# Keys on GpSimd's queue, SyncE in text order from the last q, k, v chunk on, and two low parts on GpSimd, in a gated mix of attention and MLP

## The chip, the cores and the metric

The kernel runs on one core of one Trainium2 chip. The metric is the device time of one execution in microseconds (us), smaller is better. TensorE is called PE below, VectorE DVE, ScalarE ACT, GpSimd POOL and SyncE SP. SP computes nothing here: it issues DMAs, one after the other, and where one of them has to wait, all behind it wait too. POOL both computes and issues DMAs.

## The reference

One layer norm and MLP and one attention block read the same x (2048 tokens, 448 wide) and are mixed by a gate per token:

```python
x = A_x
g = _sigmoid((x * gate_w).sum(-1, keepdims=True))
a = _A_ref(x, A_wqkv, A_wo)                    # 16 heads of 28, softmax over 2048 keys, then @ wo
b = _B_ref(x, B_w1, B_b1, B_w2, B_b2)          # layer norm, gelu(y @ w1 + b1) @ w2 + b2, 1792 wide
return g * a + (1 - g) * b
```

Everything is float32.

## The kernel before

**Products in two parts.** PE multiplies in a float32r format, so every operand is kept as a high part (ACT copies the float32 value into it) and a low part (the value minus its high part, a subtraction on DVE or POOL). A product is high times high plus the two mixed ones, and so three matmuls per tile.

**Three stages.** The tokens go in NC = 4 chunks of 512.

1. q, k, v (lines 247 to 301). Chunk c has NM = 7 tiles `qk_tile(c, m)` of 128 columns of q and k: 11 matmuls (L188) into the next of eight PSUM banks, ACT takes the high part (L190), DVE the low part (L191), and SP stores both to DRAM (L192, 512 KB). The tile `hl` that is stored has three buffers. Then come four v tiles `v_tile` (L204 on PE, L206 on ACT, L207 on DVE, stored by SP at L208, 256 KB, three buffers `vt`). Between these tiles stands other work: the layer norm's row statistics (`ln_turn`, L236 to L240), the first y of the MLP (`ln_fetch` L125 on SP; `ln_apply`: L129, L130 on POOL, L131 on ACT, L133 or L135 on POOL), and the first seven tiles of w1 (`fetch_w1` L95 on SP, `high_w1` L100 on ACT, `low_w1` L103 on DVE or POOL).
2. The MLP (lines 556 to 626). `mlp1(c, f)` for f = 0 to 13 makes 128 columns of the hidden layer: 11 matmuls (L529) into bank f % 2, two Gelus on ACT (L532, L533), the low part on POOL (L534). `mlp2` (L542, L543, L547) multiplies back, and ACT and SP store the result (L553, L554). In chunk 0 the remaining weights arrive during `mlp1`: w1 for f from 7 on, and all of w2 (`fetch_w2` L107, `high_w2` L110, `low_w2` L113), through four staging buffers (`s`, twice, and the two halves of `lnr`). Each is fetched by SP, split by ACT, and comes free when its low part is made. The list `order` gives their sequence; `stage(f)` says which are split at step f.
3. Attention: scores with their exponentials (L483, L488), products with v (L746), projection and gate.

**Row maxima as filler.** The softmax needs each row's maximum beforehand. `RowMax` makes it from the high parts alone: a matmul of q (`qd`, four DMAs at L319) with the keys (L362), and a maximum on DVE (L342, L344). `Filler` slips these products, six at a time, in banks 2 to 7, between the matmuls of the MLP from f = 4 of chunk 0 on. The keys of the first group of heads lie in `khr`; `load_khr(0)` fetches them by four DMAs (L425, 224 KB each), which wait until the k columns of all tokens have been stored by L192.

**What sets the order.** PE runs in text order everywhere. Outside a `manual_schedule` the other engines' order is planned at compile time: what a model of the times takes to be ready first comes first. Inside one the named engines run in text order. Before the change the MLP and the attention are each such a section, for SP, POOL, ACT and DVE; stage 1 is none. The planner may interleave leftovers of stage 1 with the first instructions of the MLP's section.

Of the kernel before, what the change touches and what calls it, by code (L numbers as in the profile page):

```python
# [7 lines left out]
F32 = mybir.dt.float32  # L8
# [11 lines left out]
DH = 28  # L20
# [3 lines left out]
NC = S // CH  # L24
NT = S // P
TPC = CH // P
NF = F // P
# [13 lines left out]
def kernel(ctx: ExitStack, tc: tile.TileContext, xt, wqk, wv, wo, xk, w1, b1, w2, b2,  # L41
                          ident_d, sel_d, out):
    nc = tc.nc
# [14 lines left out]
    qk = dram.tile([2, 2 * D, S], F32, name="qk")  # L58
# [13 lines left out]
    khr = mpool.tile([P, S], F32R, name="khr", bufs=1)  # L72
# [9 lines left out]
    w1h, w1l, w2h, w2l = {}, {}, {}, {}  # L82
# [8 lines left out]
    wraw = {}  # L91
# [17 lines left out]
    def high_w2(f):  # L109
        nc.scalar.activation(w2h[f], wraw[2, f], AF.Copy)  # L110

    def low_w2(f):
        nc.vector.tensor_sub(w2l[f], wraw.pop((2, f)), w2h[f].bitcast(F32))  # L113

    yh, yl = (my.tile([P, n, CH], F32R, name=f"y{n}") for n in (4, 3))
    lnr = my.tile([P, 2, CH], F32, name="lnr")
# [10 lines left out]
    def ln_apply(c, t):  # L127
        x = lnx.pop((c, t))
        nc.gpsimd.tensor_sub(x, x, lnr[:, 0])  # L129
        nc.gpsimd.tensor_mul(x, x, lnr[:, 1])  # L130
        nc.scalar.activation(yh[:, t], x, AF.Copy)  # L131
        if t < 3:
            nc.gpsimd.tensor_sub(yl[:, t], x, yh[:, t].bitcast(F32))  # L133
        else:
            nc.gpsimd.tensor_sub(yh[64:128, t], x[64:128], yh[64:128, t].bitcast(F32))  # L135


    with tc.tile_pool(name="qx", bufs=2) as qx, tc.tile_pool(name="qo", bufs=3) as qo, \
# [9 lines left out]
        def raw():  # L148
            return qx.tile([P, CH], F32, name="raw", bufs=8)

        def load_wqk(m):
            r = raw().rearrange("p (t x) -> p t x", t=4)
            nc.sync.dma_start(r, wqk[m])
            wh[m] = qw.tile([P, 4, P], F32R, name=f"wh{m}")
            wl[m] = qw.tile([P, 4, P], F32R, name=f"wl{m}")
            nc.scalar.activation(wh[m], r, AF.Copy)
            nc.gpsimd.tensor_sub(wl[m], r, wh[m].bitcast(F32))
# [8 lines left out]
        def fetch_x(c, t):  # L166
            xraw[c, t] = raw()
            nc.sync.dma_start(xraw[c, t], xt[t, :, c * CH:(c + 1) * CH])
# [76 lines left out]
            split_x(0, t)  # L245
        load_wqk(1)
        for c in range(NC):
            for m in range(NM):
                if c == 0:
                    if m + 2 < NM:  # L250
                        load_wqk(m + 2)
                    if m == 1:
                        for v in vt:
                            nc.gpsimd.memset(v[:, :, DH:DH + 1], 1.0)
                            nc.gpsimd.memset(v[:, :, DH + 1:32], 0.0)
                    if m == 3:
                        for t in range(4):
                            r = raw()[:, :450]
                            nc.sync.dma_start(r, wv[:, t])
                            nc.scalar.activation(wvh[:, t], r, AF.Copy)  # L260
                            nc.gpsimd.tensor_sub(wvl[:, t], r, wvh[:, t].bitcast(F32))
                if c + 1 < NC and m >= 3:
                    fetch_x(c + 1, m - 3)
                qk_tile(c, m)
                if c + 1 < NC and m >= 5:
                    split_x(c + 1, m - 5)
                if c == 1 and m >= 2 or c == 2 and m < 3:
                    ln_stats(m - 2 if c == 1 else m + 5)
                if c == 1 or c == 2 and m == 0:
                    stats_fetch(m if c == 1 else 7)  # L270
                if c == 1 and m == 1:
                    for t, d in ((ident, ident_d), (sel, sel_d), (b1s, b1), (ones, one_t)):
                        nc.sync.dma_start(t, d)
                if c == 1 and m == 4:
                    ln_rows(0, TPC)
                if c == 2 and m == 0:
                    ln_turn(0, TPC)
                if c == 2 and m == 2:
                    ln_load(0)
                if c == 2 and m in (3, 4, 6) or c == 3 and m == 0:  # L280
                    if c == 2 and m == 6:
                        ln_apply(0, 1)
                    ln_fetch(0, {3: 0, 4: 1, 6: 2, 0: 3}[m])
                if c == 2 and m == 5 or c == 3 and m in (1, 2):
                    ln_apply(0, 0 if c == 2 else m + 1)
                if c == 2 and m == 6:
                    ln_rows(TPC, NT)
                if c == 3 and m == 4:
                    ln_turn(TPC, NT)
                if c == 3:  # L290
                    fetch_w1(m, raw())
                    if m >= 2:
                        high_w1(m - 2)
                        low_w1(m - 2, nc.vector if m % 2 else nc.gpsimd)
            for i in range(TPC):
                if c + 1 < NC and i < 2:
                    split_x(c + 1, i + 2)
                v_tile(c * TPC + i)
                if c == 3 and i < 2:
                    high_w1(i + 5)  # L300
                    low_w1(i + 5, nc.vector if i else nc.gpsimd)
# [115 lines left out]

    khi = dict.fromkeys(range(MLP_G + 1), khr)

    def load_khr(g, k=None):  # L420

        sl = slice(0, S) if k is None else slice(k * CH, (k + 1) * CH)
        for j in range(4):
            r = D + (4 * g + j) * DH
            nc.sync.dma_start(khr[32 * j:32 * j + DH, sl].bitcast(F32), qk[0, r:r + DH, sl])  # L425

    def load_khi(g):
        if g == MLP_G:
# [125 lines left out]
        nc.sync.dma_start(gbs[c * TPC + i], gb)  # L554

    E = mybir.EngineType
    with tc.manual_schedule(engines={E.SP, E.Pool, E.Activation, E.DVE}):

        order = [x for i in range(7) for x in (NF + 7 + i, i)] + list(range(7, NF))
        def high(k):  # L560
            high_w2(k) if k < NF else high_w1(k - NF)

        def low(k):
            low_w2(k) if k < NF else low_w1(k - NF, nc.gpsimd)

        def stage(f):

            return order[max(0, 3 * (f - 1) // 2 - 1):max(0, 3 * f // 2 - 1)]

        for c in range(NC):  # L570
            for f in range(NF):
                if c == 0:
                    if f == 0:
                        stages += [lnr[:, 0], lnr[:, 1]]
                        filler.max = RowMax()
                    for k in stage(f - 1):
                        low(k)
                    for k in order[3 * f // 2:3 * (f + 1) // 2]:
                        fetch_w2(k) if k < NF else fetch_w1(k - NF, staged())
                    for k in stage(f):  # L580
                        high(k)
                    if f == 1:
                        load_khr(0)
                    if f == FS:
                        filler.spread(nc.sync, MLP_MAX, 11 * W1 * (0.8 * (NF - FS) + 3 * NF) + W2 * (3 * NF * (NT - 1) - 12))
                mlp1(c, f)
            if c == 0:
                for k in stage(NF - 1):
                    low(k)
                for k in order[3 * (NF - 1) // 2 - 1:]:  # L590
                    high(k)
                    low(k)
                stages[2:] = []
            if c == NC - 1:
                m0.close()
                aq = ctx.enter_context(tc.tile_pool(name="aq", bufs=1, side="right", reuse_waits="tile"))

                first = {3: aq.tile([P, S], F32, name="klo", bufs=2), 2: aq.tile([P, NT, P], F32, name="vg", bufs=2)}

                def early(n):  # L600
                    t = first[n] if n == 3 else first[n].rearrange("p a b -> p (a b)")
                    return t[:, :n * CH].rearrange("p (n c) -> p n c", c=CH)

                nc.scalar.activation(gate, zall, AF.Exp, scale=-1.0)
                load_khi(0)
                load_klo(0)
                load_q(0)
                load_v(0)
                load_qm(0)
            else:  # L610
                ln_load(c + 1)
                ln_fetch(c + 1, 0)
                ln_fetch(c + 1, 1)
            for i in range(TPC):
                mlp2(c, i)
                if c == NC - 1 and i == 0:
                    nc.vector.tensor_scalar_add(gate, gate, 1.0)
                    nc.vector.reciprocal(gate, gate)
                    nc.vector.tensor_scalar(ngate, gate, -1.0, 1.0, op0=OP.mult, op1=OP.add)
                if c + 1 < NC and i < 3:  # L620
                    ln_apply(c + 1, i)
                    if i < 2:
                        ln_fetch(c + 1, i + 2)
                    else:
                        ln_apply(c + 1, 3)
# [125 lines left out]
    with tc.manual_schedule(engines={E.SP, E.Pool, E.Activation, E.DVE}):  # L751
# [5 lines left out]
        for u in range(0, 4 * steps, U):  # L757
            units = list(range(u, min(u + U, 4 * steps)))
            while at < units[-1] // 4:
                at += 1  # L760
                n, k = divmod(at, NT)
                g, c = divmod(n, NC)
# [35 lines left out]
            if ended:  # L798
                n = summed // NT - 1
# [61 lines left out]
```

## Time and profile before

| | |
|---|---|
| timed runs | 1138.23, 1138.23, 1141.04 us; median 1138.23 |
| the profiled execution | 1140.1 us, of which the span is 1138.3 |
| busy in the span | PE 1114.2, DVE 739.6, ACT 633.9, POOL 327.2 us |
| mean granted PE clock | 0.993 |

The span begins with the first and ends with the last instruction that the profile shows. In it, stage 1 takes PE until about 117, the first chunk's `mlp1` until about 166, the MLP until about 475 us, and attention the rest. In a line of a timeline, the first number is the start, the second the time until the end of the last instruction merged into the line, then engine, source line, operation, output and inputs, shapes and count; in brackets stands how long the engine had been idle before, and what released it. "SPq" is SP's queue. The names are those of the tiles: `hl` of stage 1 is the pair of parts of q or k, `bank` is PSUM, `raw` a buffer for what is fetched.

### The profile page before, as it was taken

What the parts mean: (1) busy time and instruction counts of PE and PEld (TensorE: products, weight loads), DVE (VectorE), ACT (ScalarE), POOL (GpSimd) and SP (SyncE); (2) the same over time, 40 slices, a digit from 0 to 9 for tenths busy, and PEclk for the clock granted to TensorE, in tenths of its full rate; (3) what the DMA queues carried; (4) which work ended last, traced back from release to release, by engine and by line L of the source; (5) the groups of instructions that cost most, each with busy time, mean ns of one, the idle gap of its engine ahead of it and who ended that gap; (6) DMA issues with size and microseconds to landing.
All of it is one profiled execution on the core that took longest, in us unless ns stands there. A gap on an engine that the chain in (4) does not pass through costs nothing.

```text
span 1138.3 us, 19785 instructions
## 1 busy us (share of the span) xinstructions
PE 1114.2 (98%) x8136; PEld 678.9 (60%) x8136; DVE 739.6 (65%) x1031; ACT 633.9 (56%) x668; POOL 327.2 (29%) x348
## 2 busy tenths in 40 slices
PE   7999799999999999999999999999999999999996
PEld 6888677777767777744444444444444444464554
DVE  4443298888888888576666666666766766644102
ACT  5333460231131142188787887877878787747652
POOL 4006373344333332013112221221222125425140
PEclk9999899999999999999999999999999999999998
DMA  7996542010220105063100220012111102021201
GB/s 235 302 302 231 203 119 72 26 46 18 67 54 18 43 9 128 28 161 90 28 18 19 61 73 18 20 27 52 48 34 36 28 13 89 12 64 39 67 26 41
DMA packets 53055, 84.35 MB, mean 74 GB/s; under 512 B 8492, under 2 KB 28476, under 8 KB 52052
## 3 DMA queue, kind: packets, MB, share of 16 engines
q1 hardware_dynamic: 48900, 77.19, 22.5%
q0 software_dynamic: 4064, 5.89, 2.2%
q8 instruction: 64, 1.05, 0.4%
q14 instruction: 27, 0.22, 0.1%
HBM read 56.40 MB, written 26.49 MB: 73 GB/s over the span
## 4 chain that ended last, share of the span: by engine, by line
PE 94%; DMA 2%; DVE 1%; ACT 1%; issue 0%; SPq 0%; POOL 0%; ACTq 0%; DVEq 0%
PE bank L746 22%; PE bank L483 21%; PE bank L362 15%; PE bank L529 12%; PE bank L188 6%; PE bank L547 4%; PE bank L542 4%; PE bank L543 4%; PE bank L204 2%; PE bank L651 1%; PE bank L652 1%; PE bank L653 1%; DMA qk<-hl 1%; DMA raw<-in_xt 0%; DVE mx L344 0%
## 5 line engine op out<-in xcount | busy, mean ns | idle before, releaser
L488 ACT ACTIVATE pt<-bank 128x1536 f32<-128x1536 f32 (+1 forms) x408 | 482.3, 1234 | 151.5 <-PE bank L483 142.6
L342 DVE TENSOR_REDUCE mx<-bank 128x1 f32<-128x512 f32 x618 | 409.7, 687 | 175.5 <-PE bank L362 162.7
L746 PE MATMUL bank<-pt,vg 128*32 128x512 f32 x2038 | 260.9, 602 | 0.0
L344 DVE TENSOR_REDUCE mx<-bank 128x2 f32<-128x1024 f32 x203 | 238.8, 1219 | 32.5 <-PE bank L362 32.5
L362 PE MATMUL bank<-khi,qd 28*128 28x512 f32 x512 | 240.7, 479 | 0.1
L362 PEld LDWEIGHTS bank<-khi,qd 28*128 28x128 f32 x512 | 92.3, 181 | 148.1 <-DVE mx L342 105.0
L483 PE MATMUL bank<-qh,klo 28*128 28x512 f32 x1024 | 177.5, 393 | 0.0
L529 PE MATMUL bank<-y,w1f 128*128 128x512 f32 x616 | 154.1, 401 | 6.4 <-ACT h L533 6.4
L483 PE MATMUL bank<-qh,khi 29*128 29x512 f32 x768 | 160.0, 480 | 0.2 <-ACT pt L488 0.2
L529 PEld LDWEIGHTS bank<-y,w1f 128*128 128x128 f32 x616 | 113.5, 190 | 42.1 <-issue 12.3
L483 PE MATMUL bank<-ql,khi 28*128 28x512 f32 x768 | 132.3, 390 | 0.0
L534 POOL TENSOR_TENSOR hl<-h,hh 128x512 fp32r<-128x512 f32 x56 | 73.1, 1307 | 133.7 <-ACT h L533 93.0
L746 PEld LDWEIGHTS bank<-pt,vg 128*32 128x32 f32 x2038 | 45.5, 108 | 84.1 <-issue 83.3
L483 PEld LDWEIGHTS bank<-qh,klo 28*128 28x128 f32 x1024 | 89.1, 185 | 4.1
L532 ACT ACTIVATE hh<-bank,b1s 128x512 fp32r<-128x512 f32 x56 | 38.6, 689 | 88.3 <-PE bank L529 88.2
L553 ACT ACTIVATE h<-bank 128x448 f32<-128x448 f32 x16 | 8.7, 546 | 141.5 <-PE bank L547 107.5
L547 PE MATMUL bank<-w2h,hl 128*128 128x448 f32 x224 | 85.6, 382 | 0.0
L483 PEld LDWEIGHTS bank<-qh,khi 29*128 29x128 f32 x768 | 62.2, 181 | 37.6 <-ACT pt L488 33.0
L542 PE MATMUL bank<-w2h,hh 128*128 128x448 f32 x224 | 84.0, 375 | 0.0
L667 POOL DMA_DIRECT2D lt<-ob x15 | 11.0, 736 | 252.3 <-DVE ob L666 252.3
L543 PE MATMUL bank<-w2l,hh 128*128 128x448 f32 x224 | 82.5, 368 | 0.0
L362 PE MATMUL bank<-khr,qd 28*128 28x512 f32 x512 | 79.8, 466 | 1.5 <-DVE mx L344 1.5
(113 smaller groups left out, 1243.7 us busy)
## 6 DMA issues: line engine op xcount, KB each, us to landing
qk<-hl SPq DMA_DIRECT2D x28, 512.0 KB
raw<-in_xt SPq DMA_DIRECT2D x16, 256.0 KB
vs<-vt SPq DMA_DIRECT2D x16, 256.0 KB
s<-in_xt SPq DMA_DIRECT2D x16, 256.0 KB
rc<-rls POOLq DMA_DIRECT2D x60, 64.0 KB, 2.2
bxr<-in_xk SPq DMA_DIRECT2D x8, 448.0 KB
gbs<-h SPq DMA_DIRECT2D x16, 224.0 KB
klo<-qk SPq DMA_DIRECT2D x16, 224.0 KB
```

Source lines behind the costliest of these rows:

```text
L188: nc.tensor.matmul(ps, a, b, start=(i == 0), stop=(i == len(ops) - 1))
L342: nc.vector.reduce_max(self.mx[:, c0:c0 + 1], bank[:, b0], axis=AX)
L344: nc.vector.reduce_max(self.mx[:, c0:c1 + 1:c1 - c0], bank[:, b0:b1 + 1], axis=AX)
L362: nc.tensor.matmul(bank[:, b], self.qds[self.n][r, i * P:(i + 1) * P], khi[self.n // NC][r, k * 512:(k + 1) * 512], start=True, stop=True)
L483: nc.tensor.matmul(bank[:, u % U], a[r, k * P:(k + 1) * P], b[r], start=(i == 0), stop=(i == 2))
L488: nc.scalar.activation(t, bank[:, b:b + len(units)], AF.Exp, scale=SCALE)
L529: nc.tensor.matmul(ps, a, b, start=(i == 0), stop=(i == len(ops) - 1))
L534: nc.gpsimd.tensor_sub(hl[f], h, hh[f].bitcast(F32))
L542: nc.tensor.matmul(a, hh[f][:, sl], w2h[f], start=(f == 0), stop=False)
L543: nc.tensor.matmul(a, hh[f][:, sl], w2l[f], start=False, stop=False)
L547: nc.tensor.matmul(a, hl[f][:, sl], w2h[f], start=False, stop=(f == NF - 1))
L746: nc.tensor.matmul(pv[32 * j:32 * j + 32, :], vg[n // NC][:, k, 32 * j:32 * j + 32], probs.pop(4 * step + j), start=(k == 0), stop=(k == N ...
```

## The change

Three things are changed.

- `load_khr(0)` is called at f = 0 of chunk 0 instead of f = 1, and its four DMAs are issued by POOL instead of SP. In POOL's text order they stand ahead of the subtraction L534 of f = 0.
- From the last chunk (c = 3) of stage 1 on, SP is in a `manual_schedule`, which stays open until the end of the MLP and takes the place of the MLP's own for SP. So SP issues, from there on, in text order: for each m the store of q, k (L192), then what stands behind it in the loop (at m = 0 the fetch of x for t = 3 of the layer norm, at m = 4 the rows of `ln_turn`, at every m `fetch_w1(m)`), then the four stores of v, then `qd`, then the weights of `order`.
- After the `mlp1` loop of chunk 0 four w2 tiles (10 to 13) still need their low part. All four were on DVE; now the second and the fourth (tiles 11 and 13) are on POOL, behind its last L534, and the three high parts that remain are all written ahead of the low parts. On ACT the order is the same.

```diff
-    def low_w2(f):
-        nc.vector.tensor_sub(w2l[f], wraw.pop((2, f)), w2h[f].bitcast(F32))
+    def low_w2(f, lo=nc.vector):
+        lo.tensor_sub(w2l[f], wraw.pop((2, f)), w2h[f].bitcast(F32))
...
+    texts = ExitStack()
...
         for c in range(NC):
+            if c == NC - 1:
+                texts.enter_context(tc.manual_schedule(engines={mybir.EngineType.SP}))
             for m in range(NM):
...
-    def load_khr(g, k=None):
+    def load_khr(g, k=None, queue=nc.sync):
...
-            nc.sync.dma_start(khr[32 * j:32 * j + DH, sl].bitcast(F32), qk[0, r:r + DH, sl])
+            queue.dma_start(khr[32 * j:32 * j + DH, sl].bitcast(F32), qk[0, r:r + DH, sl])
...
-    with tc.manual_schedule(engines={E.SP, E.Pool, E.Activation, E.DVE}):
+    with texts, tc.manual_schedule(engines={E.Pool, E.Activation, E.DVE}):
...
-                    if f == 1:
-                        load_khr(0)
+                    if f == 0:
+                        load_khr(0, queue=nc.gpsimd)
...
             if c == 0:
-                for k in stage(NF - 1):
-                    low(k)
-                for k in order[3 * (NF - 1) // 2 - 1:]:
+                rest = order[3 * (NF - 1) // 2 - 1:]
+                for k in rest:
                     high(k)
-                    low(k)
+                for n, k in enumerate(stage(NF - 1) + rest):
+                    low_w2(k, nc.gpsimd if n % 2 else nc.vector)
```

## The prediction

> **What bounds the kernel now.** I read the page first. TensorE (PE) is busy 98% of the span and holds 94% of the chain that ended last, so only a stretch in which PE stands still, or runs at a reduced clock, can give time back; whatever such a stretch gives, the PE-bound rest passes on whole.
>
> ```profile
> PE 94%; DMA 2%; DVE 1%; ACT 1%; issue 0%; SPq 0%; POOL 0%; ACTq 0%; DVEq 0%
> ```
>
> Then I looked for PE's gaps in the busy times by stretch (columns: stretch, its length, busy PE, PE weight load, DVE, ACT, POOL with instruction counts, granted clock, DMA share, GB/s) and in PE's timeline.
>
> ```profile
> 122.00:124.00 2.00, 0.43 (x2) 0.00 (x1) 0.00 (x0) 0.00 (x0) 0.00 (x0) 1.00 1.05 407
> 124.00:126.00 2.00, 0.00 (x0) 0.00 (x0) 0.01 (x1) 0.57 (x2) 0.00 (x0) 0.74 1.04 370
> 126.00:128.00 2.00, 0.00 (x0) 0.00 (x0) 0.15 (x1) 1.99 (x3) 0.00 (x0) 0.50 0.89 285
> 128.00:130.00 2.00, 1.41 (x3) 1.16 (x4) 0.00 (x0) 2.00 (x4) 1.39 (x2) 0.50 0.88 218
> ```
> ```profile
> 117.25 5.18 PE L529 MATMUL bank<-y,w1f 128*128 128x512 f32 x22
> 128.59 10.88 PE L529 MATMUL bank<-y,w1f 128*128 128x512 f32 x40 [6.17 <-ACT h L533]
> 139.40 0.73 PE L362 MATMUL bank<-khr,qd 28*128 28x512 f32 x6
> ```
>
> PE runs the first two MLP products (f=0, 1) and stops at 122.43: f=2 reuses the PSUM bank of f=0, which ACT has not emptied. Full DMA queues and an idle core fill the hole. Its price: 6.16 us idle (122.43 to 128.59), and a restart at clock 0.5. The 40 matmuls from 128.59 to 139.40 took 10.81 us; at the pace before the hole (5.18/22 = 0.2355 us) they take 9.42. So 1.39 us of clock, 7.55 together.
>
> Why ACT is late stands in its timeline and in SP's.
>
> ```profile
> 116.67 0.60 ACT L190 ACTIVATE hl<-bank 128x512 fp32r<-128x512 f32 x1 [3.89 <-DMA qk<-hl]
> 119.12 0.60 ACT L190 ACTIVATE hl<-bank 128x512 fp32r<-128x512 f32 x1 [1.84 <-DMA qk<-hl]
> 125.42 0.54 ACT L206 ACTIVATE vt<-bank 128x448 f32<-128x448 f32 x1 [4.39 <-DMA vs<-vt]
> 125.98 1.28 ACT L532 ACT_TABLE_LOAD   x1
> ```
> ```profile
> 111.43 1.14 SPq L95 DMA_DIRECT2D lnr<-in_w  x1
> 112.67 0.52 SPq L192 DMA_DIRECT2D qk<-hl  x1
> ...
> 119.03 0.32 SPq L425 DMA_DIRECT2D khr<-qk  x1
> 119.44 1.41 SPq L192 DMA_DIRECT2D qk<-hl  x2
> 120.94 1.67 SPq L208 DMA_DIRECT2D vs<-vt  x2
> 122.66 1.12 SPq L425 DMA_DIRECT2D khr<-qk  x1
> 123.88 2.43 SPq L208 DMA_DIRECT2D vs<-vt  x2
> ```
>
> The q, k evictions (L190) have three hl buffers, the v evictions (L206) three vt buffers; each waits until an older store has landed. The hl store issued at 112.67 follows three weight fetches of the MLP (109.47 to 112.57, 0.74 MB) and lands at 119.03, 6.35 us later. SP sits on the key load L425 for it (SP's waits: 3.4 us), with the last two hl stores behind; the last vt waits 4.39 us for the first vs store; then come a table load of 1.28 us and the Gelu that frees the bank. All of ACT's q, k work was late before that: products of the last chunk start on PE at 90.3, but ACT waits 4.04 us for the layer norm's y (t=2) until 97.02 and 4.73 us for t=3 until 102.82, and its first eviction comes at 105.34.
>
> **SP in text order from chunk 3.** Stores hl 0 to 6 and vs 12 to 15 now precede the MLP's prefetches (three stood ahead, one at 127.30), and nothing of the MLP stands between them. What comes in instead is behind each hl store: the layer-norm fetch of t=3 behind the first, and one w1 fetch (256 KB) behind each; w1 was fetched between 73 and 99.5 before. Costs:
> - Bytes. From the first store to the last vs: 7 x 0.5 MB hl, 7 x 0.25 w1, 4 x 0.25 vs of this chunk and some of the chunk before, 0.25 for t=3: about 7.3 MB. The full queue moved 348 to 369 GB/s at 112 to 118, so about 20 us; started near 99 it lands near 119. The path is therefore not free of DMA, only in better order.
> - ACT. It stands at y (t=2) until 97.02 as before, then clears the v tiles left over and two hl by about 99.5. The t=3 fetch goes out near 100.4 (before: 94.57). It took 5.5 us to its reader then (100.12); I take 3 to 5.5, then two POOL ops of 1.29: y (t=3) at 106 to 108.5. Five hl follow at the queue's pace, 0.77 MB each, 2.1 us, so hl 6 near 117, the last vt near 119.5, table load, two Gelus (1.28): bank free at 122 to 125. PE wants it at 122.43. I take 1.3 us of hole left, between 0 and 3.
> - The prefetches move to after the last vs and four qd loads (0.42 each), near 121; a fetch took 2.87 us (136.83 to 139.70), so w1[7] lands near 124 to 125. ACT's high part of it stands ahead of the Gelu of f=2, which f=4 needs at 127.6: 0 to 1.5 us, I take 0.4. From there the ring of four staging buffers turns on POOL's low parts as before.
>
> A rule of the Trainium skill bears on the hole left: TensorE: Matmul & The Clock Gate, Part 1, says that the clock halves only after a whole idle window of about 3.4 us; by it a hole of 1.3 us costs 1.3. The trace half agrees: the clock was full in 122 to 124 and 0.50 from 126, but at 176.1 it fell after PE had been 0.71 to 0.76 busy for 4 us with no gap over 0.64. If any hole trips it, the 1.39 us come back and my sum is 1.4 higher.
>
> **Key loads on POOL, one step earlier.** Four loads of 224 KB leave SP (0.3 to 0.4 us each to issue, plus the 3.4 us wait). POOL DMA issues in this trace take 496 to 904 ns (L673, L667): 2.0 to 3.6 us for four. Behind them on POOL stands the subtraction L534 for f=0; POOL is idle from 107.81 to 128.62, waiting for Gelu, and the loads can go once hl 4 has landed (about 114 to 116). So nothing, between 0 and 1 (were the cover gone, the first staging buffer would come free 3 us later). The keys are first read 22 us after f=0 starts, so also late loads arrive in time. 0.9 MB are moved either way.
>
> **Two low parts on POOL.** At the end of chunk 0 four subtractions L113 stand on DVE before row maxima that PE waits for.
>
> ```profile
> 172.52 0.50 PE L362 MATMUL bank<-khr,qd 28*128 28x512 f32 x2
> 173.45 0.50 PE L362 MATMUL bank<-khr,qd 28*128 28x512 f32 x2 [0.43 <-DVE mx L344]
> 174.58 0.50 PE L362 MATMUL bank<-khr,qd 28*128 28x512 f32 x2 [0.64 <-DVE mx L344]
> ```
>
> Six such matmuls without a wait take 0.66 us; these took 2.49 (172.52 to 175.01), the six before 1.10 (168.12 to 169.22), and then the clock fell: ten matmuls in 3.59 us instead of 2.05. That is 1.83 + 0.44 + 1.54 = 3.8 us, the most there is. Two subtractions less save DVE 1.1 us (0.53 each at its pace), worth 1.1 to 2.6 with the clock. Against it: POOL and DVE take turns.
>
> ```profile
> 153.38 0.61 DVE L113 TENSOR_TENSOR w2l<-lnr,w2h 128x448 fp32r<-128x448 f32 x1
> 153.91 1.71 DVE L113 TENSOR_TENSOR w2l<-s,w2h 128x448 fp32r<-128x448 f32 x1
> ```
> ```profile
> 153.43 1.71 POOL L534 TENSOR_TENSOR hl<-h,hh 128x512 fp32r<-128x512 f32 x1 [1.83 <-ACT h L533]
> ```
>
> POOL's op, ready at 153.43, ran from 153.9, after DVE's first, and DVE's second waited until POOL was done. If POOL's low part (1.15, as L738 at 448 wide) slips between DVE's two, DVE needs 0.53 + 1.15 + 0.53 = 2.2 against 2.1 before: nothing, or -0.3. I take 0.5 of -0.3 to 3.8, near the turn-taking end, for that is the row nearest. The next layer-norm load then waits for POOL, at most 1.3 us later; its reader's result is needed at 214, its POOL work ended at 210.2, and the POOL chain in between waits for ACT's place behind the gb eviction (181.82), so that is covered.
>
> **Sum.** 7.55 - 1.3 - 0.4 - 0 + 0.5 = 6.35 us. The profiled execution has a span of 1138.3 and a time of 1140.1; the timed runs have a median of 1138.23, so I subtract from that: 1131.9. Spread of the three runs before is 0.25%; 0.3% (3.4 us) is taken as the least that tells a change.
>
> **Rivals.**
> - Half: the queue, not SP's order, sets the last vs, and a hole of 2 to 3 us with the clock stays. 7.55 - 1.39 - 0.4 less the hole is 2.8 to 3.8, with the low parts 0 to 1 more: 1133.5 to 1135.5. For: 20 us of bytes in 20 us. Against: 0.74 MB of prefetch (2.0 us at 0.36 MB per us) leave that stretch, and c=2 loses three early w1 fetches, so the layer-norm row (lnr, 6.9 us in flight at 77.94) and y may come sooner.
> - No effect: ACT's order, planned at compile time where only SP is fixed, still puts y (t=3) or a w1 high part ahead of the evictions and SP's gain is eaten: 1136 to 1140.
> - Slower, one mechanism: the t=3 fetch now stands behind the first hl store. If ACT's first eviction stays at 105.3, the fetch goes out at 107.1 rather than 94.57, y (t=3) ends at 115.3 rather than 102.82, and the six hl and four vt behind it come at 2.1 us of queue each: vt near 133 instead of 125.4. That is 7.5 us more hole: 1145.7. It decides from y (t=3) later than about 115. For it: ACT stood 4.73 us at exactly this y. Against: seven w1 high parts leave the stretch ahead of the first eviction, and SP's order forces ACT to have that eviction ahead of y.
>
> **Chances.** Forecast (1127 to 1133.5) 0.55; half 0.16, with 0.10 of it past 3.4 us; no effect 0.12; slower 0.17. Faster 0.55 + 0.10 = 0.65; within 0.06 + 0.12 = 0.18; slower 0.17. Likeliest case alone: 1127 to 1133.5. The range adds half and no effect at its top: 1126.5 (all 3.8 us of the low parts, no hole left) to 1140; left out are the slower case and a few hundredths below.
>
> **What would show it.** Right: after the last v tile PE goes from f=1 to f=2 with under 2 us of gap and clock 1.0; the last vt eviction before 120.5; L425 on POOL, none on SP between L192 and L208; no fetch into s or lnr before the last vs; f=2 starts near 123.7. The low parts: L362 groups near the end of chunk 0 without the 0.43 and 0.64 us waits, and no clock drop after. Wrong: ACT waiting for y (t=3) past 110, or PE short of a bank before the v tiles end.

## The result and the profile after

The changed kernel has a median of 1131.82 us over 18 runs (1128.15 to 1134.28), the kernel before 1138.05 over 18 (1133.22 to 1141.04): 0.995 of the time, 95% interval 0.9938 to 0.9963, 6.2 us less. The forecast was 1131.9. The number came true by luck: most of the time did not come from where the forecast had it.

The profiled execution after has a span of 1127.6 us (time 1129.41), 10.7 less than the one before. It is one of the shortest of its kernel and the one before one of the longer, so it overstates the change; a second profile of the same changed kernel is used further down (span 1133.1).

First the stretch that was to gain. PE's timeline after:

```profile
116.39 5.18 PE L534 MATMUL bank<-y,w1f 128*128 128x512 f32 x22
125.61 11.81 PE L534 MATMUL bank<-y,w1f 128*128 128x512 f32 x40 [4.04 <-ACT h L538]
137.36 0.73 PE L367 MATMUL bank<-khr,qd 28*128 28x512 f32 x6
```

and the busy times by stretch (columns as in the prediction):

```profile
122.00:124.00 2.00, 0.00 (x0) 0.00 (x0) 0.92 (x3) 1.98 (x4) 0.09 (x1) 1.00 0.92 246
124.00:126.00 2.00, 0.39 (x1) 0.39 (x2) 0.00 (x0) 1.99 (x4) 0.36 (x1) 0.51 0.81 278
126.00:128.00 2.00, 2.00 (x6) 1.52 (x6) 0.00 (x0) 0.72 (x2) 2.00 (x2) 0.50 0.45 134
130.00:132.00 2.00, 2.00 (x8) 1.59 (x7) 0.63 (x1) 1.55 (x4) 0.00 (x0) 0.78 0.43 163
```

The hole ahead of f=2 is still there: 4.04 us idle instead of 6.17, and the clock falls as before. Two later kernels run the same 40 matmuls at full clock in 9.36, so 11.81 holds 2.45 of clock; by the same measure the execution before lost 6.17 and 1.52. That is 6.5 against 7.7, a gain of 1.2 where the forecast had 5.85 (7.55 - 1.3 - 0.4). As f=0 also starts earlier here (116.39, before 117.25), the 62 products are through 2.0 us earlier.

ACT's and SP's timelines after say why:

```profile
104.88 0.63 ACT L131 ACTIVATE y<-s 128x512 fp32r<-128x512 f32 x1 [1.43 <-POOL s L130]
110.99 0.63 ACT L100 ACTIVATE w1f<-raw 128x512 fp32r<-128x512 f32 x1 [2.99 <-DMA raw<-in_w]
117.73 0.63 ACT L100 ACTIVATE w1f<-raw 128x512 fp32r<-128x512 f32 x1 [5.62 <-DMA raw<-in_w]
118.27 0.53 ACT L208 ACTIVATE vt<-bank 128x448 f32<-128x448 f32 x1
121.49 0.63 ACT L100 ACTIVATE w1f<-raw 128x512 fp32r<-128x512 f32 x1 [0.82 <-DMA raw<-in_w]
122.03 0.96 ACT L208 ACTIVATE vt<-bank 128x448 f32<-128x448 f32 x2
124.30 0.69 ACT L537 ACTIVATE hh<-bank,b1s 128x512 fp32r<-128x512 f32 x1
```
```profile
112.84 0.46 SPq L95 DMA_DIRECT2D raw<-in_w  x1
113.40 1.48 SPq L194 DMA_DIRECT2D qk<-hl  x1
114.92 0.76 SPq L95 DMA_DIRECT2D raw<-in_w  x1
118.82 5.73 SPq L210 DMA_DIRECT2D vs<-vt  x4
```

SP does what was said: no fetch into `s` or `lnr` precedes the last v store, and no key load stands on it. No eviction waits for a store any more. But ACT now waits for w1: five high parts (L100), whose fetches left SP between the last stores, stand in ACT's planned order between the evictions, and the v evictions behind them (L208) stand still for a weight that f=2 does not need. The y of t=3 was in time (104.88; forecast 106 to 108.5).

The end of chunk 0 on PE, POOL and DVE after:

```profile
171.00 1.15 PE L367 MATMUL bank<-khr,qd 28*128 28x512 f32 x4
172.77 0.50 PE L367 MATMUL bank<-khr,qd 28*128 28x512 f32 x2 [0.63 <-DVE mx L349]
```
```profile
167.30 1.54 POOL L113 TENSOR_TENSOR w2l<-lnr,w2h 128x448 fp32r<-128x448 f32 x1
168.80 1.53 POOL L113 TENSOR_TENSOR w2l<-s,w2h 128x448 fp32r<-128x448 f32 x1
```
```profile
167.19 0.64 DVE L113 TENSOR_TENSOR w2l<-lnr,w2h 128x448 fp32r<-128x448 f32 x1
167.75 1.57 DVE L113 TENSOR_TENSOR w2l<-s,w2h 128x448 fp32r<-128x448 f32 x1
```

The engines take turns as forecast: DVE's two subtractions need 0.64 + 1.57 = 2.2 us, and PE still waits 0.63 for a row maximum. In this execution the clock does not fall afterwards.

What the forecast has no term for is the end of the program. The last five stretches of the kernel before:

```profile
1128.00:1130.00 2.00, 0.91 (x5) 0.51 (x3) 1.63 (x3) 0.00 (x0) 0.00 (x0) 1.00 0.67 246
1130.00:1132.00 2.00, 0.00 (x0) 0.00 (x0) 0.00 (x0) 0.00 (x0) 0.00 (x0) 0.97 0.56 212
1132.00:1134.00 2.00, 0.00 (x0) 0.00 (x0) 0.00 (x0) 0.00 (x0) 0.00 (x0) 0.50 0.00 0
1134.00:1136.00 2.00, 0.00 (x0) 0.00 (x0) 0.00 (x0) 0.00 (x0) 0.00 (x0) 0.50 0.00 0
1136.00:1138.00 2.00, 0.00 (x0) 0.00 (x0) 0.00 (x0) 0.00 (x0) 0.00 (x0) 0.50 0.00 0
```

From 1132 to 1138 no engine computes and no byte moves. The instructions of the kernel's last line (duration in ns as least, median and longest; first and last start) and SP's waits there, before:

```profile
L856 POOLq DRAIN  x3: 40/102/10967, 1126.6 to 1138.1; - x3
```
```profile
SPq L856 <- PEq L856: 6.4, 2, 5.9
```

and after:

```profile
L861 POOLq DRAIN  x3: 40/102/1409, 1121.4 to 1127.4; - x3
```
```profile
SPq L861 <- PEq L861: 0.7, 2, 0.5
```

At the end every engine drains and meets the others. POOL's drain takes 10.97 us before; it begins at 1126.6 and ends at 1137.6, when since 1132 at the latest no byte has moved. After, it takes 1.41 and is over before the outputs are. (The view names PE's queue as the releaser; PE's own drain takes under 2 us, so the engine named is not the late one.) From the issue of the first of the last four output stores to the end of the span it is 1138.32 - 1127.83 = 10.5 us before, 1127.63 - 1122.66 = 5.0 after: 5.5 us, most of the 6.2.

### The profile page after: what moved, and what is told of

It is laid out like the page before. It is cut to its first block, busy times and chain, and to the rows that moved or that the text cites. A ratio compares the mean times of both kernels' runs of the same rounds, so it can differ in the third digit from the quotient of the medians.

```text
span 1127.6 us, 19788 instructions
## 1 busy us (share of the span) xinstructions
PE 1111.3 (99%) x8136; PEld 677.0 (60%) x8136; DVE 734.6 (65%) x1029; ACT 634.1 (56%) x668; POOL 332.0 (29%) x354
## 4 chain that ended last, share of the span: by engine, by line
PE 85%; DMA 7%; POOL 3%; DVE 2%; issue 1%; ACT 1%; SPq 1%; ACTq 0%; POOLq 0%; DVEq 0%
PE bank L751 22%; PE bank L488 20%; PE bank L367 15%; PE bank L534 11%; PE bank L552 4%; PE bank L547 4%; PE bank L548 4%; DMA raw<-in_xt 2%; DMA bxr<-in_xk 2%; PE bank L656 1%; PE bank L657 1%; PE bank L658 1%; DVE mx L349 1%; DMA s<-in_xt 1%; POOL hl L539 1%
## 5 line engine op out<-in xcount | busy, mean ns | idle before, releaser
L534 PE MATMUL bank<-y,w1f 128*128 128x512 f32 x616 | 154.9, 403 | 4.0 <-ACT h L538 4.0
L534 PEld LDWEIGHTS bank<-y,w1f 128*128 128x128 f32 x616 | 114.2, 191 | 39.6 <-issue 12.1
```

What stands on the lines that cost most here:

```text
L534: nc.tensor.matmul(ps, a, b, start=(i == 0), stop=(i == len(ops) - 1))
```

## The experiments

The kernels differ in how many DMAs POOL issues: 127 before (15 + 15 + 60 for the softmax sums, 28 `qd`, 9 `ms`), 131 after, with the four key loads. All profiles together, with "tail" as above, "idle" of PE ahead of f=2, and "hole" that idle time plus what the 40 matmuls behind it take beyond 9.36:

| kernel | median us | ratio to before, 95% | POOL DMAs | drain us | tail us | idle / hole us | clock falls at the end of chunk 0 |
|---|---|---|---|---|---|---|---|
| before | 1138.05 | 1 | 127 | 10.97 | 10.5 | 6.17 / 7.7 | yes |
| after | 1131.82 | 0.995 (0.9938 to 0.9963) | 131 | 1.41 | 5.0 | 4.04 / 6.5 | no |
| e10_after (the same) | 1131.86 | 0.9945 (0.9927 to 0.9963) | 131 | 1.41 | 5.0 | 8.75 / 10.3 | yes |
| e1_text | 1136.43 | 0.9985 (0.9968 to 1.0001) | 127 | 10.96 | 10.5 | 2.63 / 4.0 | yes |
| e2_khr | 1135.76 | 0.9966 (0.9952 to 0.9979) | 131 | 1.41 | 5.0 | 10.17 / 12.1 | yes |
| e3_low | 1135.71 | 0.9966 (0.9956 to 0.9977) | 127 | 10.96 | 10.5 | 4.82 / 7.0 | no |
| e4_text_khr | 1131.96 | 0.9940 (0.9926 to 0.9953) | 131 | 1.41 | 5.0 | 4.13 / 6.5 | no |
| e5_pad1 | 1138.98 | 1.0006 (0.9987 to 1.0026) | 128 | 11.05 | 10.6 | 5.75 / 8.5 | no |
| e9_pad2 | 1132.49 | 0.9946 (0.9927 to 0.9965) | 129 | 1.25 | 4.7 | 5.52 / 8.3 | no |
| e6_pad40 | 1133.43, one run | | 167 | 4.36 | 4.8 | 5.43 / 7.1 | yes |
| e7_early_w1 | 1130.94 | 0.9941 (0.9918 to 0.9964) | 131 | 1.41 | 5.0 | 1.47 / 1.5 | no |
| e8_early_w1_act | 1128.29 | 0.9920 (0.9895 to 0.9945) | 131 | 1.41 | 5.0 | 2.50 / 2.5 | yes |
| e11_four_vt | 1126.67 | 0.9898 (0.9876 to 0.9920) | 131 | 1.41 | 5.0 | none | no |
| e12_lows_pool | 1125.12 | 0.9882 (0.9862 to 0.9903) | 131 | 1.41 | 5.0 | none | no |

The medians of before in the sessions of the experiments lie between 1138.7 and 1139.3; each ratio is to the one of its own session.

### The parts alone

**e1_text**: only SP's text order from the last chunk on.

```diff
+            if c == NC - 1:
+                texts.enter_context(tc.manual_schedule(engines={mybir.EngineType.SP}))
...
-    with tc.manual_schedule(engines={E.SP, E.Pool, E.Activation, E.DVE}):
+    with texts, tc.manual_schedule(engines={E.Pool, E.Activation, E.DVE}):
```

> Only SP's text order from chunk 3 on; the keys stay on SP at f = 1, the four low parts on DVE. Theory A (the order of SP is the gain, through the hole before f = 2): 4 to 5.5 us faster than before (ratio 0.995 to 0.9965), the hole before f = 2 near 4 us as with the whole change, the waits of L362 at the end of chunk 0 (0.43 and 0.64 us, then a clock drop) as before. Theory B (SP's order and the low parts share the gain): 2 to 3 us faster (0.9975 to 0.998). The keys' loads now follow the first weight prefetches on SP, so nothing stands behind them that the hole waits for.

Measured: 0.9985, its interval just reaching 1: less than either theory expected. The profile has the smallest hole of this order, 4.0 us, and the long drain. So the part that was to bring nearly all brings about 1.7 us (0.15% of 1139) by the runs; the two medians lie 2.8 apart.

**e2_khr**: only the key loads, one step earlier and on POOL.

```diff
-            nc.sync.dma_start(khr[32 * j:32 * j + DH, sl].bitcast(F32), qk[0, r:r + DH, sl])
+            queue.dma_start(khr[32 * j:32 * j + DH, sl].bitcast(F32), qk[0, r:r + DH, sl])
...
-                    if f == 1:
-                        load_khr(0)
+                    if f == 0:
+                        load_khr(0, queue=nc.gpsimd)
```

> Only the four key loads on POOL at f = 0. SP loses the 3.4 us wait ahead of the last two q, k stores. Theories A and B: 0 to 1.5 us faster (ratio 0.9987 to 1.0), because the hole is set by the landing of the stores and not by SP's wait alone. A third theory, that SP's wait at the key load is the hole: 3 us or more faster, the last v eviction at 122 rather than 125.4.

Measured: 0.9966, 3.9 us, more than theories A and B gave it and not by the third. The hole of its profile, that of the slowest of its six runs, is the worst of all, 12.1: SP, rid of the key loads, issues another weight fetch (at 115.86) ahead of the last stores, and ACT's last v eviction waits 8.15 us for a store. The drain fell to 1.41: the gain comes at the other end of the program.

**e3_low**: only two of the four last low parts on POOL.

```diff
-                for k in stage(NF - 1):
-                    low(k)
-                for k in order[3 * (NF - 1) // 2 - 1:]:
+                rest = order[3 * (NF - 1) // 2 - 1:]
+                for k in rest:
                     high(k)
-                    low(k)
+                for n, k in enumerate(stage(NF - 1) + rest):
+                    low_w2(k, nc.gpsimd if n % 2 else nc.vector)
```

> Only tiles 11 and 13 of w2's low parts on POOL. Theory A: 0 to 0.5 us faster, since POOL's subtraction slips between DVE's two and DVE is done no sooner. Theory B: 1.5 to 3 us faster (ratio 0.9974 to 0.9987), the groups of six L362 at the end of chunk 0 wait less and the clock does not fall after them.

Measured: 0.9966, 3.9 us, with the long drain and the waits of 0.28 and 0.63 still in the row maxima. In its one profile the clock did not fall at the end of chunk 0. The traces show how little of the 3.9 belongs to the low parts. PE's time from the first `mlp2` matmul of chunk 0 to the first `mlp1` matmul of chunk 1, which holds the row maxima in question, is 46.1 us with two low parts on POOL and no fall of the clock (after, e3, e7, e11), 46.2 to 46.3 with all four on DVE and no fall (e4, e5, e9), and 47.6 to 47.8 in every profile with the fall, with either placing. So the placing is worth 0.1 there, the fall 1.6, and the fall comes and goes within one program (e10_after below). The rest of what sets e3's profile 4.4 us below that of before lies where nothing was changed: 1.2 us up to the end of chunk 0's `mlp1`, and 1.8 in the attention, which takes 644.9 to 645.1 us from the last MLP matmul to the last matmul in six profiles and 646.6 to 646.9 in eight. What makes the attention one or the other, the runs do not show.

**e4_text_khr**: the change without the low parts, which all stay on DVE.

```diff
-                rest = order[3 * (NF - 1) // 2 - 1:]
-                for k in rest:
+                for k in stage(NF - 1):
+                    low(k)
+                for k in order[3 * (NF - 1) // 2 - 1:]:
                     high(k)
-                for n, k in enumerate(stage(NF - 1) + rest):
-                    low_w2(k, nc.gpsimd if n % 2 else nc.vector)
+                    low(k)
```

> The change without the low parts on POOL; SP's, ACT's and PE's order are those of the whole change. Theory A: as fast as the whole change within 0.5 us (ratio to before near 0.995). Theory B: 1.5 to 3 us slower than the whole change (0.9963 to 0.9976), with the clock drop at the end of chunk 0 back.

Measured: 0.9940, where the whole change has 0.9950 and 0.9945. On top of the other two the low parts add nothing that shows (theory A). SP's order and the key loads alone add up to 0.15 + 0.34 = 0.49%, together they measured 0.60%: that fits, given their intervals. With the 0.34 of e3_low the sum would be 0.83% against 0.5% to 0.6% for the whole; the low parts' own share is what does not add.

### The drain at the end

Two explanations were left for the 5.5 us: the key loads as such (their place, their bytes), or the number of POOL's DMAs. To tell them apart, stage 1 is left as it was, and DMAs of 512 bytes into unused DRAM are added late in the attention.

**e5_pad1** (one, 128 in all) and **e6_pad40** (40 over ten steps, 167 in all); **e9_pad2** (two, 129), whose edit is shown (e5_pad1 has one at the same place, e6_pad40 four in each of ten finishes):

```diff
+    pad = [dram.tile([1, P], F32, name=f"pad{i}") for i in range(2)]
...
+        if g * NC + c == 5:
+            for _ in range(2):
+                nc.gpsimd.dma_start(pad.pop(), one_t[0:1])
```

> The kernel before with one more DMA of 512 bytes on POOL, in the attention stage: 128 POOL DMAs in the program instead of 127 (the whole change has 131). Theory C (POOL clears what it has issued once per 128 DMAs, and its last DRAIN clears the rest): the DRAIN at the end falls from 10.97 us to under 1.5, a pause of about 3 us appears on POOL at its 128th DMA, and the time falls by about 5 us (ratio near 0.9955), with nothing else moved. Theory D (it was the key loads themselves, early and large, that shortened the DRAIN): DRAIN 10.97 us and time as before.

> The kernel before with forty more such DMAs on POOL, four in each of ten finishes of the attention: 167 in all, 39 past the 128th. Theory C with a price per DMA left over ((10.97 - 1.41) / 124 = 0.077 us each): a DRAIN of 1.41 + 36 x 0.077 = 4.2 us, and the pause at the 128th. Theory C with the price falling to the least once the 128th is passed: 1.4 us. Theory D: 10.97 us or more.

> The kernel before with two more DMAs of 512 bytes on POOL: 129 in all. With 128 the DRAIN stayed at 11.05 us and with 167 it was 4.36, and in the whole change the pause stands ahead of the 129th. Theory C, mended (the 129th DMA clears the 128 before it): DRAIN near 1.25 us, a pause near 2.8 us ahead of the last of the four rc loads of the last finish, the time 5 us lower than before (ratio near 0.9955), all else as before, the hole before f = 2 too. Theory D (the key loads themselves): DRAIN 11 us, time as before.

One added DMA changes nothing (1.0006; drain 11.05): theory C had the count wrong by one. Two of them, as theory C mended has it, are worth as much as the whole change: 0.9946. POOL's timeline and drain of e9_pad2:

```profile
1077.95 1.51 POOL L674 DMA_DIRECT2D rc<-rls  x3 [1.41 <-DMA rls<-lt]
1082.14 0.50 POOL L674 DMA_DIRECT2D rc<-rls  x1 [2.68 <-issue]
1084.37 1.28 POOL L683 TENSOR_TENSOR ob<-ob,rc 128x512 f32<-128x512 f32 x1 [1.74 <-DMA rc<-rls]
```
```profile
L860 POOLq DRAIN  x3: 40/102/1250, 1126.6 to 1132.4; - x3
```

Ahead of its 129th DMA POOL stops for 2.68 us for nothing that the profile shows ("issue"); before, the four go out in one piece. In the changed kernel the stop is one DMA earlier in the same group, since there the 129th is the second of the four:

```profile
1073.09 0.52 POOL L678 DMA_DIRECT2D rc<-rls  x1 [1.41 <-DMA rls<-lt]
1076.44 1.49 POOL L678 DMA_DIRECT2D rc<-rls  x3 [2.84 <-issue]
```

The stop costs nothing: in the changed kernel POOL's next instruction waits 1.86 us longer for PE anyway, and in e9_pad2, where it starts 2.4 us later than before, the time from that group's first DMA to the last output stores is 1127.88 - 1073.06 = 54.8 us, as before (1127.83 - 1072.94 = 54.9). The drain counts what was issued since: 1 DMA 1.25 us, 3 DMAs 1.41, 39 DMAs 4.36, and without a stop 127 DMAs 10.97, 128 DMAs 11.05; (11.05 - 1.25) / 127 = 0.077 us for each. A drain of 4.36 us still costs nothing: the tail of e6_pad40, 4.8 us, is that of e9_pad2, 4.7, for the drain starts before the last output stores are issued. That it is the count is shown; what POOL does in the stop and in the drain is not. The Trainium skill (DMA: Bandwidth & Descriptors, SWDGE vs HWDGE vs iDMA) says that GpSimd writes the descriptors of its DMAs by program into rings in SBUF. Clearing such a ring would fit, but no run here shows one.

### The same kernel again

**e10_after** is the changed kernel, unaltered, for a second profile.

> The whole change again, beside the others on the same chip: ratio to before 0.994 to 0.9965, hole before f = 2 with its clock 5 to 7 us, POOL's DRAIN 1.41 us.

Its median is 1131.86. Its profile differs from the first by 5.5 us, and shows where such a spread comes from:

```profile
115.92 5.18 PE L534 MATMUL bank<-y,w1f 128*128 128x512 f32 x22
129.85 10.92 PE L534 MATMUL bank<-y,w1f 128*128 128x512 f32 x40 [8.75 <-ACT h L538]
```
```profile
176.00:178.00 2.00, 1.60 (x7) 1.28 (x8) 2.00 (x3) 0.00 (x0) 0.00 (x0) 0.90 0.90 258
178.00:180.00 2.00, 2.00 (x7) 1.79 (x6) 1.74 (x2) 0.00 (x0) 0.85 (x1) 0.50 0.22 79
```

The same instructions have a hole of 10.3 us, past the 5 to 7 expected, instead of 6.5 (ACT's five waits for w1 come to 18.5 instead of 15.3, and y is later), and the clock falls at the end of chunk 0, where it did not in the first. In this execution the last output stores are issued at 1128.11, 0.3 us later than before the change (1127.83), and the span is yet 5.2 shorter: all of it in the tail. The five profiles with the old order of stage 1 have holes of 7.7, 7.0, 8.5, 7.1 and 8.3 (mean 7.7), the four with SP in text order 4.0, 6.5, 6.5 and 10.3 (mean 6.8): about 0.9 us, within the spread. By the end of the 62 products, which also counts when f=0 starts, the means are 139.0 and 137.6: 1.4, within the spread too. And the clock fell at the end of chunk 0 in four of the seven profiles with all four low parts on DVE, and in two of the six with two on POOL.

### The hole itself

If ACT's waits for w1 make the hole, they must go with the w1 fetches out of the way. **e7_early_w1** fetches each at least three tiles earlier, still in SP's text order; **e8_early_w1_act** also puts ACT in text order from the last chunk on; **e11_four_vt** adds a fourth `vt` buffer, paid for with one of the eight `raw`. Each against the one before it, the first against the change:

```diff
-                if c == 3:
-                    fetch_w1(m, raw())
+                if c == 2 and m < 3:
+                    fetch_w1(m, raw())
+                if c == 3:
+                    if m < 4:
+                        fetch_w1(m + 3, raw())
```
```diff
-                texts.enter_context(tc.manual_schedule(engines={mybir.EngineType.SP}))
+                texts.enter_context(tc.manual_schedule(engines={mybir.EngineType.SP, mybir.EngineType.Activation}))
...
-    with texts, tc.manual_schedule(engines={E.Pool, E.Activation, E.DVE}):
+    with texts, tc.manual_schedule(engines={E.Pool, E.DVE}):
```
```diff
-        vt = [qw.tile([P, H, 32], F32, name=f"vt{i}") for i in range(3)]
+        vt = [qw.tile([P, H, 32], F32, name=f"vt{i}") for i in range(4)]
...
-            v = vt[tt % 3]
+            v = vt[tt % 4]
```

> The whole change, and the first three w1 fetches stand in chunk 2 (m = 0 to 2), the other four at m = 0 to 3 of chunk 3, three steps earlier. Theory A' (what is left of the hole before f = 2 comes from the w1 fetches between the last stores, on which ACT waits 5.05, 2.99 and 5.62 us): the last v eviction follows PE at 118 to 119, hole under 1.5 us with the clock full, 3 to 5 us faster than the whole change (ratio to before 0.990 to 0.992). Rival (the bytes of the stores set the end whatever stands between them): hole still 3 us or more and the time of the whole change.

> As the one before, and ACT too in text order from chunk 3 on. Theory A': no further gain, or 0 to 1 us, as y (t = 3) now stands behind three evictions and every w1 high part two steps behind its fetch. Rival: y (t = 3) holds the evictions of m = 3 to 6 up, the hole is 2 us or more and the time like the whole change.

> Early w1 fetches and ACT in text order as before, and a fourth vt buffer (the buffers of raw go from 8 to 7 to make room). Theory A'' (with w1 out of the way the last v eviction waits only for the first vs store, 6.03 us there, for want of a buffer): the last v eviction right after PE's last v tile, hole under 0.5 us, no drop of the clock, 3 to 4 us faster than without it and 6 to 8 faster than the whole change (ratio to before 0.987 to 0.990). Rival (the late prefetches of the MLP's weights, behind the vs stores on SP, take the place of that wait: ACT then waits for w1[7] ahead of the Gelu of f = 2): a stall of 2 to 4 us at f = 4 instead of f = 2, and at most 1.5 us faster.

e7_early_w1: the hole falls to 1.47 at full clock, but the first MLP product starts at 120.91 instead of 116.39, and the median is within a microsecond of the change. The loss has moved ahead of the MLP: in ACT's planned order the last high parts of x for chunk 3 (L177) stand behind two waits for y, PE waits 2.9 us in all for parts of x between 90 and 95, and the clock is at 0.50 from 94.9 to 98.3. With ACT's order fixed as well (e8) the start is back at 116.03, and the w1 waits are gone; what is left is the wait the kernel before had, for a v store:

```profile
113.96 0.54 ACT L208 ACTIVATE vt<-bank 128x448 f32<-128x448 f32 x1 [1.20 <-PE bank L206]
120.53 0.54 ACT L208 ACTIVATE vt<-bank 128x448 f32<-128x448 f32 x1 [6.03 <-DMA vs<-vt]
```

With the fourth buffer (e11) that one goes too, and PE runs from f=0 through 62 products:

```profile
117.32 14.48 PE L536 MATMUL bank<-y,w1f 128*128 128x512 f32 x62
131.73 0.73 PE L369 MATMUL bank<-khr,qd 28*128 28x512 f32 x6
```

1126.67 us, 0.9898. The hole and the fall of the clock are gone, as theory A'' had it, and the ratio is in its range; its steps are smaller than it expected, 5.2 us from the change (1131.86 in the same session) and 1.6 between the medians from e8_early_w1_act. With the 0.9 to 1.4 that the change had taken from the hole, the 5.2 make 6.1 to 6.6, between the 5.85 that the forecast had given to SP's order and the whole 7.55. One thing these runs do not part: the three w1 fetches that went to chunk 2 also took 0.79 MB out of the last chunk's transfers, about 2 us at the prediction's 0.36 MB per us, so a share of the gain can be bytes and not order.

### All four low parts on POOL

**e12_lows_pool**: e11 with the four subtractions all on POOL, so that none stands on DVE before the row maxima.

```diff
-                    low_w2(k, nc.gpsimd if n % 2 else nc.vector)
+                    low_w2(k, nc.gpsimd)
```

> The same, and all four of the last low parts on POOL. Theory B' (DVE's two subtractions, each waiting for POOL's turn, make the groups of L362 at the end of chunk 0 wait and the clock fall): those groups wait under 0.4 us each, no clock drop near 175, 1.5 to 3 us faster than without it. Rival (DVE is behind by then for the maxima alone): waits as before, within 0.5 us.

```profile
162.47 1.16 PE L369 MATMUL bank<-khr,qd 28*128 28x512 f32 x6
166.79 0.73 PE L369 MATMUL bank<-khr,qd 28*128 28x512 f32 x6
171.16 0.73 PE L369 MATMUL bank<-khr,qd 28*128 28x512 f32 x6
```
```profile
163.35 2.25 POOL L113 TENSOR_TENSOR w2l<-lnr,w2h 128x448 fp32r<-128x448 f32 x2
165.56 2.24 POOL L113 TENSOR_TENSOR w2l<-s,w2h 128x448 fp32r<-128x448 f32 x2
```

No group waits for a row maximum any more, and POOL, with DVE out of its way, takes 1.1 us for each instead of 1.5. It is the best kernel of the study, 1125.12 us, 0.9882 of before; its step over e11, 1.5 us, is less than the two intervals can tell apart. The traces bear it out where it should come: from the first `mlp2` matmul of chunk 0 to chunk 1 PE takes 44.4 us, in e11 46.1, with the clock full in both.

## Why the prediction was right, and where it was not

**The sum.** 7.55 - 1.3 - 0.4 - 0 + 0.5 = 6.35 against 6.2 measured. It is right by luck, through two errors that cancel: the first terms held about 1 us and not the 5.85 they say, and a term of 5.5 us is missing. Of the signs that the prediction set itself, those of SP's order came (no key load on SP, no fetch into `s` or `lnr` ahead of the last v store). Those of the gain did not: the gap was 4.04 us and not under 2, with the clock at 0.50, the last v evictions came at 122.03 and not before 120.5, f=2 started at 125.61 and not near 123.7, and the waits for row maxima stayed. The lower end of the range, by its own terms, is 1138.23 - 7.55 - 3.8 = 1126.9 and not 1126.5; nothing hangs on it.

**"7.55" and its cause: right.** The bank of f=0 was late because ACT's last evictions were; e11, without such a wait, has no hole, and its 62 products are through at 131.80 instead of 139.47, 7.7 us earlier.

**"I take 1.3 us of hole left, between 0 and 3": mis-sized.** Measured 4.0 and 8.8 us idle in two executions, and the 1.39 of clock, given back in the sum, stays (2.45 and 1.56). The step that failed is the one on ACT: the working counted the seven w1 fetches as bytes in the queue, and let the evictions follow "at the queue's pace". But ACT's order was still planned, and put each w1 high part ahead of an eviction, so evictions stood behind waits for w1 of 15.3 and 18.5 us in all. The rival "No effect" named this ("a w1 high part ahead of the evictions"), at 0.12; as a mechanism of stage 1 it is what happened, and e1_text with 0.9985 is its outcome.

**The clock.** The sum followed the rule of the Trainium skill that was cited with it (TensorE: Matmul & The Clock Gate, Part 1: a whole idle window of about 3.4 us). The traces differ from it, already the one before the change. There the stretch 124 to 126, with its 0.74, holds the fall. Cut finer:

```profile
124.00:124.90 0.90, 0.00 (x0) 0.00 (x0) 0.00 (x0) 0.00 (x0) 0.00 (x0) 1.00 1.03 389
125.00:125.90 0.90, 0.00 (x0) 0.00 (x0) 0.00 (x0) 0.48 (x1) 0.00 (x0) 0.50 1.03 348
```

The clock fell at 124.97, 2.5 us after PE stopped at 122.43; after the change it fell at 124.04, 2.5 after 121.57. In e1_text 2.63 us idle were enough, while 2.50 us in e8_early_w1_act left it at 1.00. The same page of the Trainium skill says that the window runs freely, so that the phase matters, and this the traces bear out: in every trace all changes of the granted clock lie a multiple of 3.41 us apart (before: 124.97, 131.79, 176.17, 179.58; e1_text: 123.56, 126.97, 171.34, 174.76). Counted in these stretches of 3.41 us, the clock fell behind those of stage 1 and of the hole in which PE stood idle for 1.92 us (e7_early_w1, at 94.91), 2.13, 2.16, 2.42 to 2.55 or all of it, and stayed behind 1.80 (e8_early_w1_act, whose 2.50 us are cut in two at 123.0) and 1.87 (e10_after). So here somewhat over half a stretch was enough, and the 1.39 us of clock could be lost to holes much shorter than 3.4 us. At the end of chunk 0 idle time alone does not decide: the clock fell behind stretches with 0.88 to 1.13 us idle and stayed behind some with 0.84 to 0.97; what else counts there is not shown.

**"w1[7] ... I take 0.4".** The prefetches went out at 126.43, five microseconds later than forecast, since the v stores were; the high part waited 2.41 us at 129.13, but PE, at half clock, did not wait behind it: nothing.

**Key loads on POOL: "So nothing, between 0 and 1".** In stage 1 that holds: they went out at 110.00 (two), 119.70 and 121.56, in POOL's idle time. Over the program it is the step that earned most. This is the step of the prediction that failed for the largest part of the gain: it put four more DMAs on POOL's queue at nothing, and no term covers POOL's end, which they shorten by 5.5 us. The six empty microseconds at the end stand in the profile of before, in the same kind of view by stretch that showed the hole.

**Low parts: "I take 0.5".** The turn-taking was as worked out, 2.2 us for DVE's two against 2.2 forecast, and the waits stayed (0.37 and 0.63 us, before 0.16, 0.43 and 0.64). On top of the other parts it is 0 (e4). Alone it measured 3.9, near the 3.8 named as the most, but the traces give the placing 0.1 and the fall of the clock 1.6 in that stretch; where the rest of the 3.9 in the runs comes from stays open. The clock's fall, the 1.54 in that 3.8, is no clean term: it comes and goes in executions of one program.

**"Slower".** The y of t=3 came at 104.88 and 107.42, not past 115; it did not happen.

## What to carry to other kernels

Read the last ten microseconds of a profile as closely as the middle: an empty stretch after the last output has a cause, here POOL's closing drain, which goes by the number of DMAs on POOL's queue. When an order is fixed on one engine alone, look at what the planned engines put between: a fetch that is moved also moves the wait of its reader, ahead of work that has nothing to do with it. A sum that comes true is not yet a mechanism that was right; the part left out, and the missing part done alone, showed that here.

## What the runs showed of the hardware

- POOL's closing drain takes about 0.077 us per DMA that it issued: 10.97 us for 127, 11.05 for 128. Ahead of the 129th it stops for 2.6 to 2.8 us, and the drain counts from there (1.25, 1.41 and 4.36 us for 1, 3 and 39). Up to 4.36 us of drain were hidden behind the last outputs.
- In each trace the granted clock changes only at points a multiple of 3.41 us apart. In stage 1 and at the hole it fell to 0.50 behind such a stretch with 1.92 us or more without a matmul, and stayed behind 1.87 and less. It fell also, in some executions of one program, at the end of chunk 0, where no gap is over 0.64 us.
- One program's own timing varies at one place: the same order of instructions had PE idle for 4.04 and for 8.75 us ahead of f=2.
